# Row statistics move from PSUM to SBUF, the odd heads' attention sums to other PSUM banks, and a quarter of weight granule 47 stays in PSUM

## The chip, the cores and the metric

The kernel runs on one core of one Trainium2 chip. The metric is the device time of one execution in microseconds (us). The kernel before was timed in three runs; their median is 1912.75 us, the lowest 1907.44, the highest 1921.95.

Engines are named as in the profile: PE is TensorE's matmul side and PEld its loading of weights, DVE is VectorE, ACT is ScalarE, POOL is GpSimd and SP is SyncE, which here issues the DMAs of the weights.

## The reference

The result is x + A(xn) + B(xn), where xn is the layer norm of x (2048 rows of 1024 elements, bf16). A is an attention with a recurrent memory: the sequence is cut into 64 segments of 32 rows, and each segment sees 8 memory rows that are the first 8 output rows of the segment before. So the segments can't run side by side.

```python
for s in range(n_seg):                       # 64 segments
    h = concat([mem, xn[:, 32*s:32*(s+1)]])  # 8 memory rows + 32 rows
    q, k, v = (einsum('btd,dhe->bhte', h, W) for W in (Wq, Wk, Wv))   # 32 heads of 128
    scores = einsum('bhqe,bhke->bhqk', q, k) * scale                  # 40 x 40 per head
    p = softmax(where(mask, scores, -1e9))
    o = einsum('bhte,hed->btd', einsum('bhqk,bhke->bhqe', p, v), Wo)
    mem, out_s = o[:, :8], o[:, 8:]
```

B scores each row of xn with a vector w_r, takes the two best rows, sends them through a gated network (weights 1024 x 3584 and 3584 x 1024), scales the result with the sigmoid of the score and adds it to those two rows.

## The kernel before

**Tiling.** The weights of A are cut into 64 granules of 128 x 2048 bf16 (512 KB). Granules 0 to 47 are the projections, in six phases p of eight (kc 0 to 7): q, k of the first 16 heads, q, k of the second 16, v of the first half, v of the second. Granules 48 to 63 are Wo (w = 0 to 15). 44 granules stay in SBUF (tiles wres). Twenty are streamed: read from HBM in every segment, from scratch copies (tiles wsc) that segment 0 makes, into five rotating slots (tile g). The order of the streamed ones is 2, 5, 6, 9, 13, 17, 21, 25, 29, 33, 36, 39, 42, 45, 47, 50, 53, 56, 59, 62. Two of them are partly kept in PSUM: granule 6 whole in two banks, half of 25 in a third (tiles KEPT). After segment 0 granule 6 isn't streamed at all and of 25 only 1024 columns; their kept parts are copied back to SBUF by bring_back (L350) and kept_piece (L354). keep (L333) puts a part into PSUM in segment 0: it turns 128 x 128 blocks on PE, copies them to SBUF, and turns them again.

**Order of the work.** The schedule is manual: every engine executes its instructions in the order in which the code issues them. Within a segment, PE walks through the granules; after each one, after() may issue the next fetch (SP's queue; a fetch waits until the slot's last reader is done), and the hooks stored under (p, kc) are called. A hook at (5,4) thus comes behind the matmuls of granule 44 on every engine's queue. In the hooks stand: transposes of q and k (phase + 1, kc 3), scores(0) at (2,6), exponent and soften(0) at (3,4), scores(1) at (4,6), exponent and soften(1) at (5,0), prep_left at (5,3) in some segments, attend(0,0) at (5,4) and attend(0,1) at (5,6). attend(1,0) and attend(1,1) come at w = 5 and w = 8 of Wo. The 8 last rows of the four segments of a group G (j = s mod 4) are carried on beside as "left" rows: their projections go through PSl (L647), and in segments with j = 3 Wo is also applied to them (WL). prep_left normalises them in segments with j = 3 (sum_left) and j = 0 (norm_left).

**Dependencies.** The code sets no semaphores; the framework derives them from the tiles that each instruction reads and writes.

**PSUM.** There are eight banks of 512 fp32 words per partition. Three hold KEPT. psA has two rotating banks, which phases (PSm) and Wo (WO) take in turn. psL has one for left rows. Two are fixed: BS holds the scores and probabilities (SPS, words 0 to 319), the per-row means and deviations MR (320 to 447) and ML (448 to 479); BT holds the target of transposes (PTB, words 0 to 255) and one set of attention sums (OPB, 256 to 415).

**attend.** attend(half, ph) makes, for four groups of four heads, the sums for two row quarters jl = 0 and 1. The jl = 0 sums go to WO[256:416] in the first half and to BS[0:160] in the second; the jl = 1 sums go to OPB in BT. Then copies (L591, L593) bring each set to OT and to the left rows' tile OTL: all four on ACT in the first half, jl = 0 on ACT and jl = 1 on DVE in the second. After phase 5 the residual (L269) writes WO[0:256] and norm_seg prepares the next segment's rows with MR.

**softmax.** scores (L534, L536 on PE, masks L543, L545, maximum L548, subtraction L549), exponent (L553 on ACT), soften (sum L558, reciprocal L559, products L565, L566, stream transposes L568, L569): all of L543 to L566 read or write BS. two_rows (L239, L240) fetches a mean and a deviation from MR or ML.

Of the kernel before, what the change touches and what calls it, by code (L numbers as in the profile page):

```python
# [8 lines left out]
BF16 = mybir.dt.bfloat16  # L9
F32 = mybir.dt.float32  # L10
# [7 lines left out]
N_RES = 44  # L18
N_SLOT = 5
KEPT_WHOLE = 6  # L20
KEPT_PART = 25
NEG = -30000.0

PHASES = [(0, 0), (1, 0), (0, 1), (1, 1), (2, 0), (2, 1)]
# [3 lines left out]
def kernel(  # L28
# [43 lines left out]

    NG = 64

    streamed = [2, 5, KEPT_WHOLE, 9, 13, 17, 21, KEPT_PART, 29, 33, 36, 39, 42, 45, 47, 50, 53, 56, 59, 62]
    assert len(streamed) == NG - N_RES
    n_str = len(streamed)
    resident = [g for g in range(NG) if g not in streamed]
# [28 lines left out]
    def columns(g, s):  # L107
        if s > 0 and g == KEPT_WHOLE:
            return None
        return slice(0, 1024 if s > 0 and g == KEPT_PART else 2048)  # L110

    wsc = {g: dram.tile([P, columns(g, 1).stop - columns(g, 1).start], BF16, name=f"wsc{g}")
           for g in streamed if g != KEPT_WHOLE}
# [15 lines left out]

    XS = const.tile([P, 256], BF16, name="XS")  # L130
    XN = const.tile([P, 256], BF16, name="XN")
    CT = const.tile([P, 32], F32, name="CT")
    MASK = CT[:, 0:12].bitcast(BF16)
    NEGR = CT[:, 13:14]
    V8 = CT[0:1, 16:24]
    I8 = CT[0:1, 24:32].bitcast(U32)

    BS = psS.tile([P, 512], F32, name="BS")
    BT = psT.tile([P, 512], F32, name="BT")
    SPS = BS[:, 0:8 * NK].rearrange("p (i a k) -> p i a k", i=4, a=2)  # L140
    PTB = BT[:, 0:256].bitcast(BF16)
    OPB = BT[:, 256:256 + 4 * NK]
    MR = BS[:, 320:320 + 2 * NSEG].rearrange("p (s c) -> p s c", c=2)
    ML = BS[:, 448:448 + 2 * NT].rearrange("p (t c) -> p t c", c=2)
    nc.vector.memset(SPS[:, :, :, :], 0.0)
    nc.vector.memset(XN[:, :], 0.0)
    nc.vector.memset(XS[:, :], 0.0)
# [8 lines left out]
    S6 = MISC[:, 704:704 + 24].bitcast(F32).rearrange("p (c s) -> p c s", c=2)  # L156
    RI16 = MISC[:, 728:792].bitcast(F32).rearrange("p (t c) -> p t c", c=2)
    RF = MISC[:, 792:824].bitcast(F32)
    MF = MISC[:, 824:824 + 2 * (XM + 1)].bitcast(F32)
    WRB = MISC[:, 1024:2048]  # L160
    nc.vector.memset(MF, 0.0)
# [35 lines left out]
    def spread(t0, t1):  # L197

        n = t1 - t0
        sd_rows(MV[:, t0:t1, :], VE[:, t0:t1])  # L200
        PD = OPB
        for s in range(5):
            sel = SELM[:, s, :, :].rearrange("p r g -> p (r g)") if s < 4 else SELL.rearrange("p s r g -> p (s r g)")
            nc.tensor.matmul(PD[:, 32 * s:32 * s + 2 * n], lhsT=sel, rhs=MV[:, t0:t1, :].rearrange("p t c -> p (t c)"),
                             start=(s == 0), stop=True, skip_group_check=True)
        for s in range(4):
            mr = MR.rearrange("p (t s) c -> p t s c", s=4)[0:XR4, t0:t1, s, :]
            nc.vector.tensor_copy(out=mr, in_=PD[0:XR4, 32 * s:32 * s + 2 * n].rearrange("p (t c) -> p t c", c=2))
        nc.vector.tensor_copy(out=ML[:, t0:t1, :], in_=PD[:, 128:128 + 2 * n].rearrange("p (t c) -> p t c", c=2))
        nc.vector.tensor_copy(out=RI16[:, t0:t1, 0], in_=MV[:, t0:t1, 0])  # L210
        nc.vector.reciprocal(out=RI16[:, t0:t1, 1], in_=MV[:, t0:t1, 1])

# [16 lines left out]
    def router_top():  # L229
        RROW = home(hx, [1, S], BF16, "RROW")  # L230
        nc.gpsimd.dma_start(out=RROW[:, :], in_=r_d[:, :])
        nc.vector.max(out=V8[:, :], in_=RROW[:, :])
        nc.vector.max_index(out=I8[:, :], in_max=V8[:, :], in_values=RROW[:, :])


    def two_rows(m, tag):
        n = m.shape[0]
        t = one.tile([P, 4], F32, tag=tag, name="RI")[0:n, :]
        nc.vector.tensor_copy(out=t[:, 0:1], in_=m[:, 0:1])  # L239
        nc.vector.reciprocal(out=t[:, 1:2], in_=m[:, 1:2])  # L240
        return t
# [2 lines left out]
        nc.gpsimd.dma_start(out=XN[0:XR4, :], in_=x2[s * SEG:s * SEG + XM, :].rearrange("r (g c) -> (r g) c", g=4))  # L244

    def norm_seg(s):
        mr = two_rows(MR[0:XR4, s, :], "ri")
        ab = mr[:, 2:4]
        xn = XN[0:XR4, :]
        nc.vector.tensor_scalar(out=ab[:, 0:1], in0=mr[:, 1:2], scalar1=1.0, scalar2=None, op0=ALU.add)  # L250
        nc.vector.tensor_scalar(out=ab[:, 1:2], in0=mr[:, 0:1], scalar1=mr[:, 1:2], scalar2=-1.0, op0=ALU.mult, op1=ALU.mult)
        nc.vector.tensor_scalar(out=XS[0:XR4, :], in0=xn, scalar1=ab[:, 0:1], scalar2=ab[:, 1:2],
                                op0=ALU.mult, op1=ALU.add)
        nc.vector.tensor_scalar(out=xn, in0=xn, scalar1=mr[:, 0:1], scalar2=mr[:, 1:2],
                                op0=ALU.subtract, op1=ALU.mult)
# [32 lines left out]
        return t  # L288

    def norm_left(t, G):  # L290
        mr = two_rows(ML[:, G, :], "ri")
        nc.vector.tensor_scalar(out=t[:, :], in0=t[:, :], scalar1=mr[:, 0:1], scalar2=mr[:, 1:2],
                                op0=ALU.subtract, op1=ALU.mult)

    def sum_left(t, G):

        mr = two_rows(ML[:, G, :], "ri")
        nc.vector.tensor_scalar(out=mr[:, 0:1], in0=mr[:, 0:1], scalar1=mr[:, 1:2], scalar2=-1.0,
                                op0=ALU.mult, op1=ALU.mult)
        nc.vector.tensor_scalar(out=mr[:, 1:2], in0=mr[:, 1:2], scalar1=1.0, scalar2=None, op0=ALU.add)  # L300
        nc.vector.tensor_scalar(out=t[:, :], in0=t[:, :], scalar1=mr[:, 1:2], scalar2=mr[:, 0:1],
                                op0=ALU.mult, op1=ALU.add)

    def new_stl(t):
# [7 lines left out]
    queued = []  # L312

    KEPT = [psK.tile([P, 1024], BF16, name=f"KEPT{b}") for b in range(3)]
    KEPT_COLS = {KEPT_WHOLE: {0: KEPT[0][:, 0:512], 1: KEPT[0][:, 512:1024], 2: KEPT[1][:, 0:512], 3: KEPT[1][:, 512:1024]},
                 KEPT_PART: {2: KEPT[2][:, 0:512], 3: KEPT[2][:, 512:1024]}}

    def fetch():
        if not flow:
# [14 lines left out]
    def keep(g, t):  # L334
        for c, K in KEPT_COLS[g].items():
            turned = PTB.rearrange("p (i r) -> p i r", i=4)
            for i in range(4):
                nc.tensor.transpose(out=turned[:, i, :], in_=t[:, 512 * c + P * i:512 * c + P * (i + 1)],
                                    identity=IDENT[:, :])
            XK = one.tile([P, 512], BF16, tag="vl", name="XK")  # L340
            nc.vector.tensor_copy(out=XK[:, :], in_=PTB)
            for i in range(4):
                nc.tensor.transpose(out=K[:, P * i:P * (i + 1)], in_=XK[:, P * i:P * (i + 1)], identity=IDENT[:, :])

# [156 lines left out]
    for s in range(NSEG):  # L501
# [26 lines left out]
        def scores(half):  # L528
            QKL = qkl[0]
            q, k = QT[half], KT[half]  # L530
            for il in range(4):
                for jq in range(4):
                    hh = 4 * il + jq
                    nc.tensor.matmul(SPS[32 * jq:32 * jq + 32, il, 0, :], lhsT=q[:, hh, :], rhs=k[:, hh, :],  # L534
                                     start=(il == 0), stop=True, tile_position=(0, 32 * jq), skip_group_check=True)
                    nc.tensor.matmul(SPS[32 * jq:32 * jq + XL, il, 1, :], lhsT=QKL[:, il, 2 * half, jq, :],  # L536
                                     rhs=k[:, hh, :], start=False, stop=True, tile_position=(0, 32 * jq),
                                     skip_group_check=True)
            for S4, m in ((SPS[:, :, 0, 0:XM], MASK), (SPS[:, :, 0, SEG:NK], None),
                          (SPS[:, :, 1, SEG:NK], MASK[:, 0:XL])):  # L540
                if m is not None:
                    m = m.unsqueeze(1).to_broadcast([P, 4, S4.shape[2]])
                    nc.vector.tensor_tensor(out=S4, in0=S4, in1=m, op=ALU.add)  # L543
                else:
                    nc.vector.tensor_scalar(out=S4, in0=S4, scalar1=NEGR, scalar2=None, op0=ALU.add)  # L545
            S8 = SPS.rearrange("p i a k -> p (i a) k")
            NM = one.tile([P, 8], F32, tag="nm", name="NM")
            nc.vector.tensor_reduce(out=NM[:, :], in_=S8, axis=AX.X, op=ALU.max, negate=True)  # L548
            nc.vector.tensor_tensor(out=S8, in0=S8, in1=NM[:, :].unsqueeze(2).to_broadcast([P, 8, NK]), op=ALU.add)  # L549

# [3 lines left out]

        def soften(half):
            S8 = SPS.rearrange("p i a k -> p (i a) k")
            DN = one.tile([P, 8], F32, tag="nm", name="DN")
            nc.vector.tensor_reduce(out=DN[:, :], in_=S8, axis=AX.X, op=ALU.add)  # L558
            nc.vector.reciprocal(out=DN[:, :], in_=DN[:, :])  # L559
            PT2 = one.tile([P, 2, 4, 64], BF16, tag=("bA", "bE")[half], name="PT2")  # L560
# [11 lines left out]
        def attend(half, ph):  # L572
            if half not in OT:
                OT[half] = one.tile([P, 4, 4, SEG], BF16, tag=("kt", "bC")[half], name="OT")
                if half == 0:
                    nxt["wo"] = psA.tile([P, 512], F32, tag="acc", name="WO")
                sums[half] = [BS[:, 0:4 * NK] if half else nxt["wo"][:, 256:256 + 4 * NK], OPB]
            PTm, PTl = PTs[half]
            for il in range(4):
                for jl in range(2):  # L580
# [43 lines left out]
        if s > 0:  # L624
            hook(0, 0, lambda: bring_back(3, nc.scalar.copy))
            if j in (2, 3):
                hook(0, 1, lambda: bring_back(0, nc.vector.tensor_copy))
            hook(2, 1, lambda: kept_piece(KEPT_PART, 2, nc.vector.tensor_copy))
            hook(2, 2, lambda: kept_piece(KEPT_PART, 3, nc.vector.tensor_copy))
            hook(1, 5, turn_lx)  # L630
        hook(2, 6, lambda: scores(0))
        hook(3, 4, exponent)
# [182 lines left out]
    free_homes += [-1] * N_SLOT  # L815
    fetch_moe()
    assert not moe
    T0 = one.tile([P, 1024], BF16, tag="vl", name="T0")
    XS = T0[0:2, :]
    T1 = one.tile([P, 1024], BF16, tag="otl", name="T1")  # L820
# [107 lines left out]
```

## Time and profile before

| what | value |
|---|---|
| median of 3 runs | 1912.75 us |
| the profiled execution | 1914.95 us |
| its span | 1913.2 us |
| PE busy | 1607.9 us, 84% of the span |
| DVE busy | 906.8 us, 47% |
| ACT busy | 703.0 us, 37% |
| moved by DMA | 712.39 MB, mean 372 GB/s |
| HBM read, written | 694.32 MB, 22.29 MB |
| fetches of whole streamed granules | 1134, each 512 KB |
| fetches of half of granule 25 | 63, each 256 KB |

In the rows that follow, a timeline row gives start, duration, engine, line, operation, tile written <- tiles read, shape, and in brackets the idle time of the engine just before it and what ended it. A group's row gives the count, total busy time and mean duration in ns, and then the idle time before its members. A row of waits gives who waited, for whom, the sum, how often, and the longest. "DMA g<-wsc" is the fetch of a streamed granule. Since matmuls are pipelined, their ends are modelled.

### The profile page before, as it was taken

To read this page: it belongs to the slowest core of one execution; us is meant where nothing else is said; L and a number is where in the kernel's file an instruction comes from. 1 tells how busy PE (TensorE), PEld (TensorE's weight loads), DVE (VectorE), ACT (ScalarE), POOL (GpSimd) and SP (SyncE) were. 2 spreads that over 40 slices of the span, in tenths; PEclk is the share of its full clock that TensorE was granted. 3 is DMA by queue.
4 is the path that set the end of the run, shared out by engine and by line. 5 is a ranking of instruction groups with operands and counts; after the bars stand their busy time and mean duration, and the time that the engine had idled before them with its cause. 6 is when DMAs were issued, how large, how long until landed. Compare 5 with 4: busy or idle time off the path is not lost. (4 is left out here: it accounts for less than half of the span.)

```text
span 1913.2 us, 82718 instructions
## 1 busy us (share of the span) xinstructions
PE 1607.9 (84%) x36320; PEld 891.0 (47%) x36320; DVE 906.8 (47%) x2884; ACT 703.0 (37%) x1886; POOL 294.0 (15%) x590
## 2 busy tenths in 40 slices
PE   3558898888889888989889898989888898889864
PEld 1224545444454445545454554545454544545443
DVE  6824544554455445444554454445444544455430
ACT  1113433443334343434344343334333443343320
POOL 2201111111110211112111111211121111111110
PEclk8669999999999999999999999999999999999995
DMA  9999999999999999999999999999999999999998
GB/s 369 399 363 378 358 381 365 380 379 354 383 352 390 350 382 376 378 381 369 387 353 373 370 372 362 362 387 365 370 363 384 376 366 385 365 386 368 393 390 330
DMA packets 224441, 712.39 MB, mean 372 GB/s; under 512 B 33664, under 2 KB 44464, under 8 KB 224080
## 3 DMA queue, kind: packets, MB, share of 16 engines
q1 hardware_dynamic: 194384, 671.18, 92.9%
q0 software_dynamic: 21056, 28.07, 4.4%
q10 hardware_dynamic: 8640, 7.87, 1.2%
q8 instruction: 283, 4.64, 0.9%
q14 instruction: 78, 0.64, 0.1%
HBM read 694.32 MB, written 22.29 MB: 375 GB/s over the span
## 5 line engine op out<-in xcount | busy, mean ns | idle before, releaser
L669 PE MATMUL PSm<-wres,ST 128*32 128x512 bf16 x8448 | 720.2, 385 | 21.2 <-DVE ST L283 6.7
L669 PEld LDWEIGHTS <-ST 128*32 128x32 bf16 x12288 | 325.8, 96 | 396.4 <-issue 166.9
L669 PE MATMUL PSm<-g,ST 128*32 128x512 bf16 x3588 | 362.4, 387 | 88.5 <-DMA g<-wsc 60.3
L685 ACT CAST XB<-PSm 128x512 bf16<-128x512 f32 x256 | 150.0, 586 | 306.9 <-PE PSm L669 305.3
L730 PEld LDWEIGHTS <-OT 128*32 128x32 bf16 x8192 | 214.1, 97 | 104.1 <-issue 80.8
L730 PE MATMUL WO<-wres,OT 128*32 128x256 bf16 x5632 | 237.2, 275 | 14.0 <-issue 8.9
L647 PE MATMUL PSl<-wres,STL 128*32 128x512 bf16 x2112 | 200.3, 390 | 1.5 <-issue 1.4
L526 DVE COPY KT<-BT 128x512 bf16<-128x512 bf16 x128 | 52.5, 410 | 307.7 <-ACT XB L685 148.9
L458 POOL DMA_DIRECT2D LX<-ql_d x63 | 33.8, 537 | 937.6 <-ACT OTL L593 525.0
L730 PE MATMUL WO<-g,OT 128*32 128x256 bf16 x2560 | 131.2, 279 | 54.4 <-DMA g<-wsc 42.0
L793 POOL DMA_DIRECT2D out_dram<-XN x256 | 129.6, 514 | 228.0 <-DVE XN L791 219.1
L707 ACT CAST VM<-PSm 128x512 bf16<-128x512 f32 x128 | 77.0, 602 | 153.5 <-PE PSm L669 121.5
L350 ACT COPY BK<-KEPT 128x512 bf16<-128x512 bf16 x126 | 78.3, 621 | 96.9 <-PE WO L730 96.9
L521 ACT COPY QT<-BT 128x512 bf16<-128x512 bf16 x128 | 75.0, 586 | 105.3 <-PE BT L516 99.7
L647 PEld LDWEIGHTS <-STL 128*32 128x32 bf16 x3072 | 85.1, 98 | 57.7 <-issue 8.0
L584 PEld LDWEIGHTS <-VM 32*128 32x128 bf16 x2048 | 67.6, 91 | 93.0 <-issue 71.3
L516 PEld LDWEIGHTS <-XB 128*128 128x128 bf16 x1024 | 58.5, 98 | 106.1 <-ACT XB L685 76.7
L543 DVE TENSOR_TENSOR BS<-BS,CT 128x96 f32<-128x96 f32 (+1 forms) x256 | 59.7, 233 | 100.8 <-PE BS L536 96.3
L354 DVE COPY g<-KEPT 128x512 bf16<-128x512 bf16 x126 | 47.6, 420 | 122.5 <-PE PSm L669 70.2
L791 DVE CAST XN<-WO 128x256 bf16<-128x256 f32 x64 | 27.2, 425 | 160.7 <-PE WO L730 160.7
L516 PE MATMUL BT<-IDENT,XB 128*128 128x128 bf16 x1024 | 102.0, 222 | 1.4 <-ACT QKL L476 1.4
L558 DVE TENSOR_REDUCE DN<-BS 128x8 f32<-128x320 f32 x128 | 63.0, 492 | 67.2 <-ACT BS L553 67.2
(168 smaller groups left out, 2382.2 us busy)
## 6 DMA issues: line engine op xcount, KB each, us to landing
g<-wsc SPq DMA_DIRECT2D x1134, 512.0 KB, 6.1
g<-wsc SPq DMA_DIRECT2D x63, 256.0 KB, 5.5
LX<-ql_d POOLq DMA_DIRECT2D x63, 128.0 KB, 6.0
ql_d<-XBl ACTq DMA_DIRECT2D x60, 128.0 KB, 5.6
MW<-in_B_w_gate_dram SPq DMA_DIRECT2D x16, 448.0 KB, 9.2
MW<-in_B_w_up_dram SPq DMA_DIRECT2D x16, 448.0 KB, 9.1
wres<-in_A_Wk_dram SPq DMA_DIRECT2D x12, 512.0 KB, 14.3
MW<-in_B_w_down_dram SPq DMA_DIRECT2D x12, 512.0 KB, 10.2
```

What stands on the lines that cost most here:

```text
L350: copy(out=back[c][:, :], in_=KEPT_COLS[KEPT_WHOLE][c])
L516: nc.tensor.transpose(out=PTq[:, il, :, :].rearrange("p j r -> p (j r)"), in_=XB[:, il * P:(il + 1) * P], identity=IDENT[:, :])
L521: nc.scalar.copy(out=QT[half][:, :, :], in_=pv)
L543: nc.vector.tensor_tensor(out=S4, in0=S4, in1=m, op=ALU.add)
L558: nc.vector.tensor_reduce(out=DN[:, :], in_=S8, axis=AX.X, op=ALU.add)
L584: nc.tensor.matmul(o, lhsT=VM[half][q0:q0 + 32, il * P:(il + 1) * P], rhs=PTm[q0:q0 + 32, il, 0:NK], start=True, stop=False, tile_position ...
L647: nc.tensor.matmul(PSl[32 * jq:32 * jq + 32, :], lhsT=STL[:, g % KC, :], rhs=part(Gv, jq), start=first_, stop=last_, tile_position=(0, 32 ...
L669: nc.tensor.matmul(PSm[32 * jq:32 * jq + 32, :], lhsT=ST[:, kc, :], rhs=part(Gv, jq), start=(kc == 0), stop=(kc == KC - 1), tile_position= ...
L685: nc.scalar.copy(out=XB[:, :], in_=PSm[:, :])
L707: nc.scalar.copy(out=VM[half][:, :], in_=PSm[:, :])
L730: nc.tensor.matmul(PS[32 * g:32 * g + 32, 0:256], lhsT=lhs(h), rhs=Gv[:, D * hs + 256 * g:D * hs + 256 * (g + 1)], start=False, stop=(last ...
L793: nc.gpsimd.dma_start(out=out2[s * SEG:s * SEG + XM, 256 * g:256 * (g + 1)], in_=OB[32 * g:32 * g + XM, :])
```

## The change

Four things change together.

- MR leaves BS. The statistics of segments 1 to 63 lie in SBUF as bf16 (MRS, in the tile CT), those of segment 0 in MR0; ML stays in BS, but as bf16 in 16 words (480 to 495). The small tiles of two_rows and of the softmax (RI, NM, DN) become fixed places in CT. The two best scores and their places wait in BS (TOP, words 496 to 511) until the end.
- OPB moves from BT to BS[320:480].
- attend's sums: jl = 0 go to OPB in both halves; jl = 1 go to WO[256:416] in the first half and to a bank of their own from psA (SUM) in the second. Which engine copies which jl stays.
- The freed 256 words of BT keep the last quarter of granule 47 as bf16. In segment 0 keep puts it there; from segment 1 on the fetch of 47 brings 1536 of its 2048 columns, and a DVE copy at (4,5) brings the rest.

```diff
-KEPT_PART = 25
+KEPT_PARTS = {25: (2, 3), 47: (3,)}
...
-        return slice(0, 1024 if s > 0 and g == KEPT_PART else 2048)
+        return slice(0, 2048 - 512 * len(KEPT_PARTS.get(g, ())) if s > 0 else 2048)
...
-    CT = const.tile([P, 32], F32, name="CT")
+    CT = const.tile([P, 25 + NSEG - 1], F32, name="CT")
...
+    MRS = CT[:, 13:13 + NSEG - 1].bitcast(BF16).rearrange("p (s c) -> p s c", c=2)
+    RI = CT[:, 12 + NSEG:16 + NSEG]
+    NM = CT[:, 16 + NSEG:24 + NSEG]
...
-    OPB = BT[:, 256:256 + 4 * NK]
-    MR = BS[:, 320:320 + 2 * NSEG].rearrange("p (s c) -> p s c", c=2)
-    ML = BS[:, 448:448 + 2 * NT].rearrange("p (t c) -> p t c", c=2)
+    OPB = BS[:, 320:320 + 4 * NK]
+    ML = BS[:, 480:480 + NT].bitcast(BF16).rearrange("p (t c) -> p t c", c=2)
+    TOP = BS[0:1, 496:512]
...
-    def two_rows(m, tag):
-        n = m.shape[0]
-        t = one.tile([P, 4], F32, tag=tag, name="RI")[0:n, :]
+    def two_rows(m):
+        t = RI[0:m.shape[0], :]
...
-        mr = two_rows(MR[0:XR4, s, :], "ri")
+        mr = two_rows(MRS[0:XR4, s - 1, :] if s else MR0[0:XR4, :])
...
+    KEPT_COLS = {47: {3: BT[:, 256:512].bitcast(BF16)}, KEPT_WHOLE: {0: KEPT[0][:, 0:512], 1: KEPT[0][:, 512:1024], 2: KEPT[1][:, 0:512], 3: KEPT[1][:, 512:1024]},
...
-            NM = one.tile([P, 8], F32, tag="nm", name="NM")
...
-            DN = one.tile([P, 8], F32, tag="nm", name="DN")
+            DN = NM
...
-                sums[half] = [BS[:, 0:4 * NK] if half else nxt["wo"][:, 256:256 + 4 * NK], OPB]
+                beside = psA.tile([P, 512], F32, tag="acc", name="SUM")[:, 0:4 * NK] if half else nxt["wo"][:, 256:256 + 4 * NK]
+                sums[half] = [OPB, beside]
...
+            hook(4, 5, lambda: kept_piece(47, 3, nc.vector.tensor_copy))
...
+    T3 = one.tile([P, 16], F32, tag="bA", name="T3")
+    V8 = T3[0:1, 0:8]
+    I8 = T3[0:1, 8:16].bitcast(U32)
+    nc.vector.tensor_copy(out=V8, in_=TOP[:, 0:8])
+    nc.vector.tensor_copy(out=I8, in_=TOP[:, 8:16])
```

More of the change, by code (lines that the diff above doesn't have):

```diff
@@ L73 @@
     NG = 64
-    streamed = [2, 5, KEPT_WHOLE, 9, 13, 17, 21, KEPT_PART, 29, 33, 36, 39, 42, 45, 47, 50, 53, 56, 59, 62]
+    streamed = [2, 5, KEPT_WHOLE, 9, 13, 17, 21, 25, 29, 33, 36, 39, 42, 45, 47, 50, 53, 56, 59, 62]
     assert len(streamed) == NG - N_RES
@@ L131 @@
     XN = const.tile([P, 256], BF16, name="XN")
-    CT = const.tile([P, 32], F32, name="CT")
+    CT = const.tile([P, 25 + NSEG - 1], F32, name="CT")
     MASK = CT[:, 0:12].bitcast(BF16)
-    NEGR = CT[:, 13:14]
-    V8 = CT[0:1, 16:24]
-    I8 = CT[0:1, 24:32].bitcast(U32)
+    NEGR = CT[:, 12:13]
+    MRS = CT[:, 13:13 + NSEG - 1].bitcast(BF16).rearrange("p (s c) -> p s c", c=2)
+    RI = CT[:, 12 + NSEG:16 + NSEG]
+    NM = CT[:, 16 + NSEG:24 + NSEG]
     BS = psS.tile([P, 512], F32, name="BS")
@@ L158 @@
     RF = MISC[:, 792:824].bitcast(F32)
+    MR0 = MISC[:, 880:882]
+    MLT = MISC[:, 884:884 + 2 * NT]
     MF = MISC[:, 824:824 + 2 * (XM + 1)].bitcast(F32)
@@ L206, in spread @@
         for s in range(4):
-            mr = MR.rearrange("p (t s) c -> p t s c", s=4)[0:XR4, t0:t1, s, :]
-            nc.vector.tensor_copy(out=mr, in_=PD[0:XR4, 32 * s:32 * s + 2 * n].rearrange("p (t c) -> p t c", c=2))
-        nc.vector.tensor_copy(out=ML[:, t0:t1, :], in_=PD[:, 128:128 + 2 * n].rearrange("p (t c) -> p t c", c=2))
+            pd = PD[0:XR4, 32 * s:32 * s + 2 * n].rearrange("p (t c) -> p t c", c=2)
+            if t0 == 0 and s == 0:
+                nc.vector.tensor_copy(out=MR0[0:XR4, :], in_=pd[:, 0, :])
+                pd = pd[:, 1:, :]
+            if pd.shape[1]:
+                a = 4 * (t0 + (t0 == 0 and s == 0)) + s - 1
+                nc.vector.tensor_copy(out=MRS[0:XR4, a:a + 4 * (pd.shape[1] - 1) + 1:4, :], in_=pd)
+        nc.vector.tensor_copy(out=MLT[:, 2 * t0:2 * t1], in_=PD[:, 128:128 + 2 * n])
+        nc.vector.tensor_copy(out=BS[:, 480 + t0:480 + t1], in_=MLT[:, 2 * t0:2 * t1].bitcast(F32))
         nc.vector.tensor_copy(out=RI16[:, t0:t1, 0], in_=MV[:, t0:t1, 0])
@@ L231, in router_top @@
         nc.gpsimd.dma_start(out=RROW[:, :], in_=r_d[:, :])
+        V8 = home(hm, [1, 8], F32, "V8")
+        I8 = home(resident[-3], [1, 8], U32, "I8")
         nc.vector.max(out=V8[:, :], in_=RROW[:, :])
         nc.vector.max_index(out=I8[:, :], in_max=V8[:, :], in_values=RROW[:, :])
-    def two_rows(m, tag):
-        n = m.shape[0]
-        t = one.tile([P, 4], F32, tag=tag, name="RI")[0:n, :]
+        nc.vector.tensor_copy(out=TOP[:, 0:8], in_=V8[:, :])
+        nc.vector.tensor_copy(out=TOP[:, 8:16], in_=I8[:, :])
+    def two_rows(m):
+        t = RI[0:m.shape[0], :]
         nc.vector.tensor_copy(out=t[:, 0:1], in_=m[:, 0:1])
@@ L290, in norm_left @@
     def norm_left(t, G):
-        mr = two_rows(ML[:, G, :], "ri")
+        mr = two_rows(ML[:, G, :])
         nc.vector.tensor_scalar(out=t[:, :], in0=t[:, :], scalar1=mr[:, 0:1], scalar2=mr[:, 1:2],
@@ L295, in sum_left @@
     def sum_left(t, G):
-        mr = two_rows(ML[:, G, :], "ri")
+        mr = two_rows(ML[:, G, :])
         nc.vector.tensor_scalar(out=mr[:, 0:1], in0=mr[:, 0:1], scalar1=mr[:, 1:2], scalar2=-1.0,
@@ L314 @@
     KEPT = [psK.tile([P, 1024], BF16, name=f"KEPT{b}") for b in range(3)]
-    KEPT_COLS = {KEPT_WHOLE: {0: KEPT[0][:, 0:512], 1: KEPT[0][:, 512:1024], 2: KEPT[1][:, 0:512], 3: KEPT[1][:, 512:1024]},
-                 KEPT_PART: {2: KEPT[2][:, 0:512], 3: KEPT[2][:, 512:1024]}}
+    KEPT_COLS = {47: {3: BT[:, 256:512].bitcast(BF16)}, KEPT_WHOLE: {0: KEPT[0][:, 0:512], 1: KEPT[0][:, 512:1024], 2: KEPT[1][:, 0:512], 3: KEPT[1][:, 512:1024]},
+                 25: {2: KEPT[2][:, 0:512], 3: KEPT[2][:, 512:1024]}}
     def fetch():
@@ L339, in keep @@
                                     identity=IDENT[:, :])
-            XK = one.tile([P, 512], BF16, tag="vl", name="XK")
+            XK = one.tile([P, 512], BF16, tag="bx" if "vl" in group else "vl", name="XK")
             nc.vector.tensor_copy(out=XK[:, :], in_=PTB)
@@ L627 @@
                 hook(0, 1, lambda: bring_back(0, nc.vector.tensor_copy))
-            hook(2, 1, lambda: kept_piece(KEPT_PART, 2, nc.vector.tensor_copy))
-            hook(2, 2, lambda: kept_piece(KEPT_PART, 3, nc.vector.tensor_copy))
+            hook(2, 1, lambda: kept_piece(25, 2, nc.vector.tensor_copy))
+            hook(2, 2, lambda: kept_piece(25, 3, nc.vector.tensor_copy))
+            hook(4, 5, lambda: kept_piece(47, 3, nc.vector.tensor_copy))
             hook(1, 5, turn_lx)
```

## The prediction

> **What bounds the kernel now.** First the page, to see which resource is full:
>
> ```profile
> span 1913.2 us, 82718 instructions
> PE 1607.9 (84%) x36320; PEld 891.0 (47%) x36320; DVE 906.8 (47%) x2884; ACT 703.0 (37%) x1886; POOL 294.0 (15%) x590
> ...
> DMA  9999999999999999999999999999999999999998
> ...
> q1 hardware_dynamic: 194384, 671.18, 92.9%
> ...
> L669 PE MATMUL PSm<-g,ST 128*32 128x512 bf16 x3588 | 362.4, 387 | 88.5 <-DMA g<-wsc 60.3
> ...
> L730 PE MATMUL WO<-g,OT 128*32 128x256 bf16 x2560 | 131.2, 279 | 54.4 <-DMA g<-wsc 42.0
> ...
> g<-wsc SPq DMA_DIRECT2D x1134, 512.0 KB, 6.1
> ```
>
> The DMA engines are busy in every slice, and a granule lands 6.1 us after its issue; yet PE shows only 60.3 + 42.0 = 102.3 us of waiting for streamed granules, 1.62 us in each of 63 segments. So DMA and PE run close to each other, and a saving on one side counts only up to where the other takes over. Next the windows, cut near the middle of segment 25 and where segment 26 begins (columns: stretch, length, busy time of PE, PEld, DVE, ACT, POOL, clock, DMA share, GB/s):
>
> ```profile
> 799.00:816.00 17.00, 15.39 (x410) 8.87 (x402) 10.76 (x35) 7.20 (x22) 0.54 (x1) 1.00 1.01 386
> 816.00:826.00 10.00, 8.64 (x138) 3.59 (x130) 1.84 (x6) 3.54 (x7) 2.71 (x6) 1.00 0.98 363
> ```
>
> The second part of a segment moves 386 GB/s and the first part of the next 363: the transfers set the pace late in a segment, where streamed granules stand closer together, and have some slack early.
>
> Then the order of work around attend(0,0), segment 25 (timelines of DVE, PE and ACT):
>
> ```profile
> 804.29 0.39 DVE L526 COPY KT<-BT 128x512 bf16<-128x512 bf16 x1
> 805.23 0.27 DVE L543 TENSOR_TENSOR BS<-BS,CT 128x96 f32<-128x96 f32 x1 [0.56 <-PE BS L536]
> 807.58 0.49 DVE L558 TENSOR_REDUCE DN<-BS 128x8 f32<-128x320 f32 x1 [0.49 <-ACT BS L553]
> 808.68 0.21 DVE L566 TENSOR_TENSOR OTL<-BS,DN 128x64 bf16<-128x64 f32 x1
> ...
> 807.20 0.19 PE L584 MATMUL BT<-PT,VM 32*128 32x40 bf16 x1
> 809.29 0.31 PE L269 MATMUL WO<-XS,IDENT 128*32 128x256 bf16 x4 [0.20 <-ACT OTL L593]
> ...
> 807.12 0.42 ACT L553 ACTIVATE BS<-BS 128x320 f32<-128x320 f32 x1 [1.03 <-DVE BS L549]
> 808.93 0.30 ACT L593 CAST OTL<-WO 128x32 bf16<-128x32 f32 x1
> 809.23 0.31 ACT L593 CAST OTL<-BT 128x32 bf16<-128x32 f32 x1
> ```
>
> Two things are to be seen. PE starts the first half's attention sums at 807.20, into BT, while ACT (from 807.12) and DVE (until 808.68 + 0.21 = 808.89) still work on the second half's scores in BS. And PE's residual, which writes words 0 to 255 of WO, starts at 809.29, 0.06 us after ACT has read words 256 to 415 of the same WO (808.93 + 0.30 = 809.23): a write waits for a read of **other words of the same PSUM tile**.
>
> **The change part by part.**
>
> *The lighter transfer.* Granule 47 is read in 1536 of 2048 columns in 63 segments: 128 KB less each. At the 386 GB/s of the late part, where it lands, that is 131072 / 386e3 = 0.34 us, 21 us in all. It is worth this only where PE waits for DMA afterwards.
>
> *Its copy from PSUM.* The trace has the same copy for granule 25, and the pieces of keep for the once-only turning in segment 0:
>
> ```profile
> L354 DVE COPY g<-KEPT 128x512 bf16<-128x512 bf16 x126 | 47.6, 420 | 122.5 <-PE PSm L669 70.2 <-DMA g<-wsc 31.1 <-PE PSl L647 21.2
> L343 PE MATMUL KEPT<-IDENT,XK 128*128 128x128 bf16 x24 | 3.0, 264 | 5.7 <-DVE XK L341 5.7
> L338 PE MATMUL BT<-IDENT,g 128*128 128x128 bf16 x24 | 2.9, 258 | 0.0
> ```
>
> One copy is 0.42 us. It stands on DVE's queue between the copy to KT, which ends at 804.29 + 0.39 = 804.68, and the first mask at 805.23, which waits for PE's scores: a gap of 0.55 us hides it. Its slot was granule 33's, which PE has passed before the transposes that KT waits for; so it finds nothing to wait for. Without that cover, masks, softmax and what follows come 0.1 to 0.4 us later per segment, 6 to 25 us; I take 0 and keep 10 for the range. Turning the piece in segment 0 costs (3.0 + 5.7 + 2.9) / 6 pieces = 1.9 us of PE, under the loads of the weights, and that segment also copies 128 KB less to the scratch; together I take 0, with 2 us either way.
>
> *Odd heads' sums.* attend(0,0) writes jl = 0 into BS instead of WO, and jl = 1 into WO instead of BT. OPB and SPS are views of the one tile BS. If the wait seen in WO holds here, PE can't start before the last read of BS that stands earlier in the program: ACT's exponential and all of DVE's softmax up to L566; in the segments with j = 3 and j = 0 also the two reads of ML in BS (L239, L240) that prep_left puts at (5,3), behind two stream transposes. Segment 25 above, and the next three (for each the DVE read that ends last and PE's start):
>
> ```profile
> 835.97 0.21 DVE L566 TENSOR_TENSOR OTL<-BS,DN 128x64 bf16<-128x64 f32 x1
> 834.34 0.19 PE L584 MATMUL BT<-PT,VM 32*128 32x40 bf16 x1
> ...
> 863.45 0.15 DVE L240 RECIPROCAL RI<-BS 128x1 f32<-128x1 f32 x1
> 860.86 0.19 PE L584 MATMUL BT<-PT,VM 32*128 32x40 bf16 x1
> ...
> 890.73 0.15 DVE L240 RECIPROCAL RI<-BS 128x1 f32<-128x1 f32 x1
> 889.36 0.19 PE L584 MATMUL BT<-PT,VM 32*128 32x40 bf16 x1
> ```
>
> With 0.06 us from a read's end to PE's start, the new stall is 808.89 + 0.06 - 807.20 = **1.75** us in segment 25 (j = 1), 1.90 in 26 (j = 2), 2.80 in 27 (j = 3) and 1.58 in 28 (j = 0): 2.01 on the mean. The row of L269 shows ACT as the reader. If only ACT held PE up, the stall would end with the exponential, 807.12 + 0.42 + 0.06 - 807.20 = 0.40 us. The code names no engine in this, so I take the long value and keep 0.40 for the range. [...]
>
> Behind the waiting matmul on PE's queue are granules 45 and 47, the rest of attend(0), the residual and all of Wo. ACT's copies of the sums and of VM wait for PE, and so does SP, whose next fetches need the slots that PE frees.
>
> *The order in WO.* ACT now copies the sums in BS first and those in WO second, so the residual waits for the last of its four copies: 809.23 + 0.31 = 809.54 instead of 809.23, another **0.31** us. Where PE comes later anyway it costs less, at the least nothing.
>
> *What covers it.* A late PE doesn't wait where it waited before. PE's waits from attend(0,0) to about 6 us into the next segment, from the waits in these four stretches (us in total, times, longest):
>
> ```profile
> PE PSm L669 <- DMA g<-wsc: 1.3, 3, 0.7
> PE WO L730 <- DMA g<-wsc: 0.8, 2, 0.7
> PE BS L584 <- ACT VM L707: 0.4, 1, 0.4
> ...
> PE WO L730 <- DMA g<-wsc: 1.8, 3, 0.8
> PE PSm L669 <- DMA g<-wsc: 0.4, 1, 0.4
> ...
> PE WL L269 <- DVE VL L712: 0.7, 1, 0.7
> ...
> PE WO L730 <- DMA g<-wsc: 1.0, 2, 0.8
> ...
> 805.00 0.40 PE L669 MATMUL PSm<-g,ST 128*32 128x512 bf16 x4
> 805.21 0.40 PE L669 MATMUL PSm<-wres,ST 128*32 128x512 bf16 x4
> ```
>
> The last two rows show what a wait hides: a set of four matmuls counts as busy for 0.40 us, but the next starts after 0.21, so each listed wait is about 0.19 us longer than its idle time. Stall (with the 0.31) against cover: segment 25: 2.06 against 1.3 + 0.8 + 0.4 + 5 x 0.19 = 3.45, nothing left; 26: 2.21 against 2.2 + 4 x 0.19 = 2.96, nothing left; 27: 3.11 against 0.7, 2.4 left; 28: 1.89 against 1.0 + 2 x 0.19 = 1.38, 0.5 left. Where cover is left over (25 and 26), DMA still sets the end and the 0.34 counts. The four together: 2.4 + 0.5 - 2 x 0.34 = 2.2 us, or 0.56 per segment, **35 us** in 63.
>
> Against that stands the mean of the run, from its list of waits:
>
> ```profile
> PE PSm L669 <- DMA g<-wsc: 60.3, 125, 1.3
> ...
> PE WO L730 <- DMA g<-wsc: 42.0, 104, 1.2
> ```
>
> 1.62 us of waits, plus 0.19 x (125 + 104) / 63 = 0.69, is 2.31 per segment against a stall of 2.01 + 0.31 = 2.32. Were all of it usable, nothing would remain of the stall and nothing of the gain: 0, and with the extra 0.31 gone as well -20. It isn't all usable: a part lies ahead of the attention, and segment 27, with the longest stall and WL's second set of projections, has hardly any. I take +23, two thirds of the way from 0 to 35.
>
> *The rest.* two_rows reads SBUF instead of PSUM, NM and DN share one place: small DVE operations of 0.1 to 0.2 us each, with norm_seg off PE's path; 0. The top-two copies through PSUM are a few such operations once, in segment 0 and beside the last weights' loads; 0, at most 1 us.
>
> **The sum.** 1914.95 (the profiled execution, 1.75 above its span) + 23 = 1938; the median of the three runs is 2.2 lower, so against it **1936**. One per cent, 19 us, is about what a measurement tells from no change, as the three runs themselves spread over 14.5 us.
>
> **The rivals.**
>
> 1. *DMA swallows the stall* (other side: not slower). If DMA is the bound over the whole cycle, the 2.3 us only take the place of PE's waits, and each segment ends 0.34 us earlier: 1912.75 - 21 = 1892. For it: the full DMA row, and 2.31 against 2.32. Against it: PE waits for no granule in segment 27's list. It decides where cover exceeds 2.32 + 0.34 us in nearly every segment. 0.12; with cover just meeting the stall, 1903 to 1922, another 0.15.
> 2. *No wait arises* (disjoint words of BS aren't ordered, or DVE doesn't count and the stall is 0.40, wholly covered): also 1892. The L269 row speaks against the first. 0.05.
> 3. *The stall is hardly covered.* A late PE frees slots late, SP issues late, and DMA idles in turn, so that waits come back further on: from half of 2.32 x 63 = 146 us less the relief, 1912.75 + 73 - 21 = 1965, towards 1990. For it: the first part of a segment, at 363 GB/s, already isn't full. Against it: 6.1 us to landing, at 512 KB / 386e3 = 1.36 us for one granule, means about four in flight, far more than 2.8 us of stall. 0.15.
> 4. *The change doesn't do what it says:* the copy into granule 47's slot waits for that granule's own transfer and blocks DVE's queue. Landing after 6.1 instead of 0.55 us would delay the masks by 5.5 us per segment, 346 us: 2260. Some of L354's idle time ends with a DMA (31.1 us), but the copies for granule 25 don't take that long. 0.03.
>
> The forecast itself has 0.50, with 1922 to 1955 as its own range.
>
> **How the numbers follow.** Below 1894 lie most of rivals 1 (its first half) and 2: faster 0.10. Above 1932 lie three quarters of the forecast and rivals 3 and 4: slower 0.55. The rest, 0.35, is within 1%. The range from 1897 to 1970 leaves out about 0.1 on each side.
>
> **What would show it.** Right: the first L584 of attend(0,0) writes BS 0.06 us behind L566 (j = 1, 2) or L240 (j = 3, 0), with PE idle some 1.5 to 3 us before it; L269 follows ACT's last copy; the waits for g<-wsc in L730 fall well below 42 us; q1 moves 8 MB less, and DMA's share drops under that of before. Wrong: L584 starts while DVE still reads BS; the waits of L730 stay; the L354 copy at (4,5) ends after the first mask could start; or the segments with j = 3 are not the ones that grow.

## The result and the profile after

The changed kernel takes 2048.7 us (median of 4 runs, 2045.6 to 2050.7) against 1913.9 us: a ratio of **1.070, 95% interval 1.066 to 1.075**, 135 us slower. The profiled execution has a span of 2044.0 us. The forecast had the sign, but not the size; the measured time lies far above its range of 1897 to 1970, and above the 1990 up to which its third rival reached.

The lines of the page of the changed kernel that answer to those shown of before:

```profile
span 2044.0 us, 82818 instructions
PE 1649.5 (81%) x36328; PEld 919.5 (45%) x36328; DVE 928.0 (45%) x2954; ACT 698.3 (34%) x1886; POOL 292.8 (14%) x590
...
DMA  9999999999999999999999999999999999999998
...
q1 hardware_dynamic: 194384, 662.92, 89.6%
...
L682 PE MATMUL PSm<-g,ST 128*32 128x512 bf16 x3588 | 369.5, 396 | 105.5 <-DMA g<-wsc 88.5
...
L596 PE MATMUL BS<-PT,VM 32*128 32x40 bf16 x1024 | 94.2, 181 | 131.6 <-DVE CT L252 80.8
```

q1 moves 8.3 MB less, as it should, but the span is 131 us longer. The last row is the new stall: PE sits idle for 131.6 us ahead of attend's sums in BS, 10.0 us of them once, in segment 0. Note the DMA row: nines in all slices but the last, as before, although the mean rate has fallen from 372 to 344 GB/s. A slice is 51 us long, almost two segments, and a 9 stands for 90% or more, so the row hides stretches as slack as those shown below, at 68 to 82%; it doesn't say that the transfers are what the others wait for.

The list of waits of the changed kernel (us in total, times, longest), who held PE:

```profile
PE PSm L682 <- DMA g<-wsc: 88.5, 125, 2.8
PE BS L596 <- DVE CT L252: 80.8, 31, 10.0
...
PE BS L596 <- DVE OTL L577: 50.8, 33, 2.1
PE WO L281 <- ACT OTL L605: 22.9, 59, 0.5
...
PE WO L743 <- DMA g<-wsc: 4.5, 12, 0.7
```

Before, the residual's row was this:

```profile
PE WO L269 <- ACT OTL L593: 4.6, 23, 0.2
```

In 33 segments the stall ends with DVE's L577, the last product of the softmax (L566 before), in 31 with L252, the read of ML (L240 before). The waits for granules in Wo have nearly vanished (42.0 before, 4.5 now). But those in the projections have grown from 60.3 to 88.5. The new copy of granule 47's last quarter never waits, neither for PE nor for its own transfer:

```profile
L366 DVE COPY g<-BT 128x512 bf16<-128x512 bf16 x63 | 25.8, 409 | 0.0
```

Segment 27 (j = 3) in both timelines and in five stretches. First the end of the stall, DVE's row and PE's:

```profile
916.31 0.15 DVE L252 RECIPROCAL CT<-BS 128x1 f32<-128x1 bf16 x1
...
916.51 0.17 PE L596 MATMUL BS<-PT,VM 32*128 32x40 bf16 x1 [3.22 <-DVE CT L252]
```

PE starts 0.05 us behind DVE's last read of BS. Now the windows up to the middle of the stall, in the rest of it, to the point where the clock changes, while it is changed, and to the segment's end (length, busy PE, PEld, DVE, ACT, POOL, clock, DMA share, GB/s):

```profile
896.30:914.60 18.30, 16.41 (x298) 7.77 (x299) 8.30 (x25) 6.16 (x13) 3.56 (x7) 0.91 1.01 371
914.60:916.50 1.90, 0.00 (x0) 0.00 (x0) 1.76 (x9) 0.00 (x0) 0.00 (x0) 1.00 1.01 386
916.50:917.80 1.30, 1.19 (x32) 0.62 (x32) 0.71 (x3) 0.77 (x4) 0.00 (x0) 0.99 0.68 274
917.80:921.20 3.40, 3.13 (x62) 2.32 (x65) 1.78 (x7) 1.19 (x5) 0.00 (x0) 0.50 0.74 196
921.20:926.60 5.40, 5.40 (x190) 4.33 (x182) 2.06 (x7) 2.03 (x7) 0.52 (x1) 1.00 0.82 269
```

Here two things are to be seen that the prediction hadn't. While PE stands still, DMA goes on at 386 GB/s for a while, but then falls to 274, 196 and 269: the transfers that were already issued run out, and new ones are issued only as PE frees slots: in this segment's trace SP issues no fetch between 913.22 and 917.26 us. SP's queue bears this out over the whole run; before, and then with the change, it waited for PE's projections and for PE's Wo:

```profile
SPq L327 <- PE PSm L669: 446.9, 593, 2.7
...
SPq L327 <- PE WO L730: 136.8, 249, 1.8
```

```profile
SPq L339 <- PE PSm L682: 552.5, 612, 4.0
...
SPq L339 <- PE WO L743: 200.4, 249, 1.8
```

And 1.3 us after the stall **PE's clock falls to 0.50 for 3.4 us**. A set of eight matmuls of Wo then takes about twice as long: the next set starts 0.43 us later in the slow stretch and 0.23 us later after it.

```profile
919.97 0.67 PE L743 MATMUL WO<-g,OT 128*32 128x256 bf16 x8
920.40 0.67 PE L743 MATMUL WO<-wres,OT 128*32 128x256 bf16 x8
...
921.97 0.40 PE L743 MATMUL WO<-g,OT 128*32 128x256 bf16 x8
922.20 0.39 PE L743 MATMUL WL<-g,OTL 128*32 128x256 bf16 x8
```

In the trace of the changed kernel the clock stands at 0.5 in 45 stretches, 181 us together, leaving out the first 150 us and one long stretch behind the last segment; before it was 4 stretches and 17 us. 39 of the 45 begin between 0.9 us before and 2.8 us after the start of attend(0,0). The mean granted clock:

```profile
core 0: 2044.0 us, clock 0.924
```

It was 0.961 before. After segment 0, all 15 segments in which PE was idle for 2.39 us or more ahead of attend(0,0) saw such a stretch, and 22 of the 38 with 1.3 to 2.4 us. What decides between these can be read from the same trace: in it every change of the clock lies on a grid of 3.41 us, and each of the 45 stretches is one or two steps of it long. Of the steps at full clock between 160 and 1700 us, all 20 in which PE was busy for less than 47% of the time were followed by a slow one, 16 of 52 with 47 to 65%, and none of 336 with more (busy time by the modelled ends of the matmuls). So in this trace it counts how much of an idle time falls into one step.

### The profile page after: what moved, and what is told of

It reads as the page before. It is cut to its first block, busy times and chain, and to the rows that moved or that the text cites. A ratio compares the mean times of both kernels' runs of the same rounds, so it can differ in the third digit from the quotient of the medians.

```text
span 2044.0 us, 82818 instructions
## 1 busy us (share of the span) xinstructions
PE 1649.5 (81%) x36328; PEld 919.5 (45%) x36328; DVE 928.0 (45%) x2954; ACT 698.3 (34%) x1886; POOL 292.8 (14%) x590
## 3 DMA queue, kind: packets, MB, share of 16 engines
q1 hardware_dynamic: 194384, 662.92, 89.6%
## 5 line engine op out<-in xcount | busy, mean ns | idle before, releaser
L682 PE MATMUL PSm<-g,ST 128*32 128x512 bf16 x3588 | 369.5, 396 | 105.5 <-DMA g<-wsc 88.5
L743 PE MATMUL WO<-wres,OT 128*32 128x256 bf16 x5632 | 265.1, 305 | 5.0 <-DMA wres<-in_A_Wo_dram 3.2
L743 PEld LDWEIGHTS <-OT 128*32 128x32 bf16 x8192 | 231.1, 106 | 45.9 <-issue 21.0
L596 PE MATMUL BS<-PT,VM 32*128 32x40 bf16 x1024 | 94.2, 181 | 131.6 <-DVE CT L252 80.8
L603 ACT CAST OT<-BS 128x128 bf16<-128x128 f32 x256 | 67.9, 265 | 368.9 <-PE WO L598 187.9
L743 PE MATMUL WO<-g,OT 128*32 128x256 bf16 x2560 | 142.2, 299 | 11.8 <-DMA g<-in_A_Wo_dram 6.8
L598 PEld LDWEIGHTS <-VL 32*128 32x128 bf16 x2048 | 71.6, 94 | 138.8 <-issue 138.7
L596 PEld LDWEIGHTS <-VM 32*128 32x128 bf16 x2048 | 75.1, 93 | 92.5 <-issue 88.2
L603 DVE CAST OT<-SUM 128x128 bf16<-128x128 f32 x128 | 37.3, 291 | 145.2 <-PE SUM L598 145.2
```

Of the source, the lines that this page charges most:

```text
L596: nc.tensor.matmul(o, lhsT=VM[half][q0:q0 + 32, il * P:(il + 1) * P], rhs=PTm[q0:q0 + 32, il, 0:NK], start=True, stop=False, tile_position ...
L598: nc.tensor.matmul(o, lhsT=group["vl"][q0:q0 + 32, c0:c0 + P], rhs=PTl[q0:q0 + 32, il, 0:NK], start=False, stop=True, tile_position=(q0, 0 ...
L603: copy(out=OT[half][:, 2 * ph + jl, :, :], in_=ov[:, :, 0:SEG])
L682: nc.tensor.matmul(PSm[32 * jq:32 * jq + 32, :], lhsT=ST[:, kc, :], rhs=part(Gv, jq), start=(kc == 0), stop=(kc == KC - 1), tile_position= ...
L743: nc.tensor.matmul(PS[32 * g:32 * g + 32, 0:256], lhsT=lhs(h), rhs=Gv[:, D * hs + 256 * g:D * hs + 256 * (g + 1)], start=False, stop=(last ...
```

## The experiments

After the result three causes were open for 135 us: the stall with the slow clock (A), the stall with DMA running dry (B), and something else in the change. A ratio is always to the kernel before, on the same chip.

**The stall taken away (e1), and the lighter transfer with it (e2).** BT's words 0 to 159 are free in phase 5, so the first half's jl = 0 sums can go there:

```diff
-                sums[half] = [OPB, beside]
+                sums[half] = [OPB if half else BT[:, 0:4 * NK], beside]
```

> The changed kernel, but the first half's jl = 0 sums go to BT, words 0 to 159 (free at that time), instead of BS; nothing else differs. All theories in which the wait for BS is the cause (the stall with the clock, or the stall with starved DMA): PE starts attend(0,0) without the wait of about 2 us, PE's clock falls to half no more often than before (4 stretches after the first 150 us, against 45 in the changed kernel), and the time is 1892 if the lighter transfer counts whole (-21 us), up to 1914 if it counts for nothing. If something else in the change is the cause (SUM in the rotating banks, the DVE copy at (4,5)), it stays above 1990.

> The same as e1_sums_in_bt, but granule 47 is streamed whole as before. This leaves the moved statistics, SUM, and BT for the first half: 1908 to 1920, the time before. The difference to e1_sums_in_bt is what the lighter transfer is worth without a stall: 21 us if DMA sets the pace in every segment, 10 to 15 if in half of them, under 5 if PE does.

e1: 1926.0 us, ratio 1.0066 (1.0035 to 1.0097). e2: 1934.4 us, 1.0094 (1.0065 to 1.0124). In e1's list of waits no L596 waits for DVE's softmax any more, and the clock is 0.952; it is at half in 11 stretches, 41 us together, not in 4 as was expected. So the wait for BS is the cause of about 122 of the 135 us. But 12 us remain in a kernel that has no stall and moves less, 20 us in the one that moves as much as before. Both lie outside what was expected: a third cause is left. The lighter transfer is worth 8 us here by the medians, 5 by the ratios, not 21, and the intervals overlap.

**PE kept busy during the stall (e3).** The work fills the gap, and its result is overwritten by the residual and the sums:

```diff
             PTm, PTl = PTs[half]
+            if half == 0 and ph == 0:
+                for n in range((7, 6, 6, 12)[j]):
+                    for jq in range(4):
+                        nc.tensor.matmul(nxt["wo"][32 * jq:32 * jq + 32, :], lhsT=ST[:, n % KC, :],
+                                         rhs=res_tiles[44][:, 512 * jq:512 * (jq + 1)], start=True, stop=True,
+                                         tile_position=(0, 32 * jq), skip_group_check=True)
```

> The changed kernel, with 6 or 7 sets (12 where j = 3) of four matmuls on PE ahead of attend(0,0), 1.3 to 2.6 us of work whose result isn't used, just long enough to fill most of the stall. Theory A (the idle PE is put to half clock for 3.4 us, 181 us in all against 17 before, and that costs up to half of the 164 us and eats the cover): half clock falls below 60 us and the time falls by 50 to 82 us, to 1965 to 2000. Theory B (a PE that frees its slots late starves DMA, the clock is a side effect): the time stays within 10 us of 2049, whatever the clock does.

2022.5 us, ratio 1.057 (1.054 to 1.060). The clock's mean is 0.954, 51 us in slow stretches, counted as above. PE is as late as in the changed kernel, but awake:

```profile
PE PSm L688 <- DMA g<-wsc: 80.9, 126, 2.4
...
PE BS L602 <- DVE CT L252: 17.5, 15, 10.7
...
PE BS L602 <- DVE OTL L577: 11.4, 25, 0.8
```

Of the 17.5 us in the second row 10.7 are segment 0. Both theories miss: the clock costs about 1.31% or **25 us**, by the intervals 15 to 35, neither 50 to 82 nor nothing. The larger part, 5.0% between e1 and e3 or 96 us, is the late PE itself. The wait in segment 0 has little part in this: attend(0,0) of segment 1 starts at 151.3 us in e1's trace and at 151.8 in e3's.

**The changed kernel without the lighter transfer (e4).** Granule 47 is streamed whole:

```diff
-KEPT_PARTS = {25: (2, 3), 47: (3,)}
+KEPT_PARTS = {25: (2, 3)}
...
-            hook(4, 5, lambda: kept_piece(47, 3, nc.vector.tensor_copy))
```

> The changed kernel with granule 47 streamed whole, so with the stall but without the lighter transfer and the DVE copy. If the stall has made PE the bound: 2045 to 2057, the lighter transfer worth under 8 us. If DMA still sets the pace (theory B): 2065 to 2072, 21 us more.

2049.5 us, ratio 1.072 (1.068 to 1.076) against 1.070 (1.066 to 1.075): with the stall in place, 8.3 MB less and the DVE copy together make no difference that can be measured. This is the first branch: under the stall it isn't the amount of the transfers that sets the pace.

**The order of the sums (e5, e6).** e1 still has the jl = 0 sums outside WO, so that the residual waits for ACT's last copy. e5 turns them round:

```diff
-                sums[half] = [OPB if half else BT[:, 0:4 * NK], beside]
+                sums[half] = [OPB, beside] if half else [beside, BT[:, 0:4 * NK]]
```

> As e1_sums_in_bt, but in the first half jl = 0 goes to WO and jl = 1 to BT, the order of before; so ACT frees WO two copies earlier and the residual needn't wait for the last of them. Theory order (the residual's wait is what e1_sums_in_bt still loses): the stretch from attend(0,0) to the residual falls by 0.2 to 0.3 us, the time by 13 to 20 us, to 1906 to 1913. Theory other (moved statistics, SUM, or DVE's extra copy cost it): within 5 us of e1_sums_in_bt's 1926.

> As e5_wo_first, with granule 47 streamed whole: what is left of the change are the moved statistics and SUM. Theory order: 1912 to 1918, the time before. Theory other: 1925 to 1935. The difference to e5_wo_first is again the lighter transfer alone: 8 us by the first pair, 21 if DMA set the pace everywhere.

e5: 1932.7 us, 1.0062 (1.0037 to 1.0087); e6: 1930.1 us, 1.0064 (1.0039 to 1.0088), where the kernel before took 1919.5 on that chip. The theory of the order falls. Nor does this pair show a gain from the lighter transfer: 0.0002 between the ratios. The residual's wait did shrink, from e1's row to e5's:

```profile
PE WO L281 <- ACT OTL L605: 26.2, 60, 0.5
```

```profile
PE WO L281 <- ACT OTL L605: 7.7, 39, 0.2
```

But 18.5 us of PE's waiting went and the time stayed: these 0.3 us are covered. And e6, which has nothing of the change left but the moved statistics with the longer CT and the other places of the sums, SUM among them, still loses 0.64%.

**PE made late (e7).** e5 with three sets of the extra matmuls, range(3), ahead of each attend(0,0).

> As e5_wo_first, with 3 sets of four matmuls (0.65 us of PE, result not used) ahead of each attend(0,0): PE comes 0.65 us later in 64 segments, 41 us, but is never idle, so the clock stays. Theory cover (a late PE only loses waits it had anyway, 1.6 us and more per segment): 0 to 8 us above e5_wo_first. Theory starved DMA (slots come free later, so the transfers come later by as much): 30 to 41 us above.

1957.6 us, ratio 1.0198 (1.0167 to 1.0229), 24.9 us above e5, of 41 us inserted: 60% comes through. Between the two theories, nearer to starved DMA.

**prep_left behind the attention (e8).**

```diff
-            hook(5, 3, prep_left)
+            hook(5, 7, prep_left)
```

> The changed kernel with prep_left at (5,7) instead of (5,3), behind attend(0,0) and attend(0,1) on all queues. If the reads of ML in BS (behind two stream transposes) are what makes the stall longer where j = 3 and j = 0: the stall there falls by 0.9 us where j = 3 (3.26 to about 2.3) and by 0.3 to 0.9 where j = 0, about 20 to 35 us in all with what the clock adds: 2014 to 2030. If not, 2045 to 2052.

2013.1 us, ratio 1.050 (1.047 to 1.053), 2.0% or 38 us less than the changed kernel. The stall no longer ends with a read of ML:

```profile
PE BS L596 <- DVE OTL L577: 58.4, 45, 2.2
PE BS L596 <- DVE BX L577: 30.4, 16, 2.3
...
PE BS L596 <- DVE BS L246: 11.9, 1, 11.9
```

The last row is segment 0. Without that segment it is 88.8 us of idle PE instead of 121.6, and the mean distance from the matmul before to attend(0,0) falls from 3.26 to 2.25 us where j = 3 and from 2.15 to 1.22 where j = 0. With the clock (0.930 against 0.924) the gain is slightly more than was expected.

**The third cause: where the slots lie (e9, e10, e11).** A 4096-byte packet of a granule took 160 ns or less in 88% of all cases before, but in 56 to 63% in every one of these kernels with the change (counted from the trace's packets of q1 between 160 and 1700 us). What all of these share is the longer table CT, 88 words instead of 32, which stands ahead of the streamed slots in SBUF: they begin 224 bytes further on in each partition, at byte 198880 instead of 198656. The shift follows from the sizes of CT; the addresses themselves stand in no trace. e11 is the kernel before with nothing but a longer CT; e9 is e5, and e10 the changed kernel, with the slots back in their place (CT keeps 32 words, the other statistics go behind all tiles):

```diff
-    CT = const.tile([P, 32], F32, name="CT")
+    CT = const.tile([P, 72], F32, name="CT")
```

```diff
-    CT = const.tile([P, 25 + NSEG - 1], F32, name="CT")
+    CT = const.tile([P, 32], F32, name="CT")
+    CU = rest.tile([P, NSEG - 8], F32, name="CU")
```

> The kernel before with one edit: CT has 72 words instead of 32, of which 40 are unused, so that every slot g starts 160 bytes further on. Nothing else of the change is in it. Theory address: the share of quick packets falls from 88% to about 56 to 63% and the time rises by 8 to 15 us, ratio 1.004 to 1.008. Theory statistics: ratio 1.000, within 0.2%.

> As e5_wo_first (no stall, the order of before, the lighter transfer), but the larger table of statistics no longer stands ahead of the streamed slots in SBUF: CT keeps its 32 words, 56 words of statistics go behind all other tiles, so every slot g starts again at byte 198656, as before, and not 224 bytes further. Theory address (in before 88% of the 4096-byte packets took 160 ns or less, in every kernel with the longer CT 56 to 63%): the share returns to about 88%, the 12 us that e5_wo_first and e6_wo_first_no47 lose vanish and the lighter transfer shows: ratio to before 0.987 to 1.000. Theory statistics (the moved statistics or SUM cost it): ratio 1.004 to 1.009 as in e5_wo_first.

> The changed kernel with its slots back at byte 198656, by the same edit: the stall stays. Theory address: 8 to 15 us faster than the changed kernel, ratio to before 1.062 to 1.066. Theory statistics: ratio 1.068 to 1.073 as measured.

e11: 1930.0 us, ratio **1.0058** (1.0031 to 1.0086): an unused 160 bytes per partition cost 11 us. Its share of quick packets is 71%, higher than was expected, and its page shows the same packets and bytes as before:

```profile
span 1934.3 us, 82718 instructions
...
q1 hardware_dynamic: 194384, 671.18, 92.8%
```

92.8% of 16 x 1934.3 us over 194384 packets is 147.8 ns for one, counting all sizes; before it was 92.9% of 16 x 1913.2, 146.3 ns.

e9: 1910.3 us, ratio **0.9958** (0.9933 to 0.9983), 88% quick packets: without the stall and with its slots in place the rest of the change is 8 us faster than before, and 1.04% faster than e5. e10: 2038.9 us, 1.0618 (1.0570 to 1.0665), 0.8% below the changed kernel, about as expected, though the two intervals touch; its share is 86%. So the theory of the statistics falls: it is the place of what lies behind CT. CT moves everything behind it; that the streamed slots are what counts is argued from the packets alone. Only shifts of 160 and 224 bytes were run, and why the place matters isn't shown.

**As late as the stall, but awake and in place (e12).** e9 with nine sets, range(9), ahead of each attend(0,0).

> As e9_aligned, with 9 sets of four matmuls (1.94 us of PE, result not used) ahead of each attend(0,0): PE is late by about what the stall made it, 124 us in 64 segments, but never idle, so the clock stays. Theory cover (only what exceeds the waits for DMA costs): 20 to 45 us above e9_aligned. Theory starved DMA (in e7_plus3 25 of 41 us came through, 60%): 75 to 110 us above.

1998.7 us, 88.5 us above e9, of 124 us inserted: 71%. What PE waits for granules in e9, and then in e12:

```profile
PE PSm L687 <- DMA g<-wsc: 61.5, 118, 1.9
...
PE WO L748 <- DMA g<-wsc: 33.0, 73, 2.2
```

```profile
PE PSm L693 <- DMA g<-wsc: 61.5, 94, 2.1
...
PE WO L754 <- DMA g<-wsc: 27.1, 41, 2.0
```

94.5 us against 88.6: a PE that comes 1.94 us later in every segment still waits nearly as long for its granules. SP's queue tells why, first in e9, then in e12:

```profile
SPq L344 <- PE PSm L687: 460.2, 608, 2.8
SPq L344 <- DMA g<-wsc: 320.7, 578, 2.7
```

```profile
SPq L344 <- PE PSm L693: 574.1, 612, 6.2
SPq L344 <- DMA g<-wsc: 258.8, 425, 2.6
```

The fetches wait 114 us longer for the matmuls of the projections to free their slots, so they are issued later.

## Why the prediction was right or wrong

The 135 us come apart by differences of ratios, times 1914 us: 96 the late PE (e3 against e1), 25 the clock (the changed kernel against e3), 20 the place of the slots (e5 against e9; e10 gives 16, and e11 gives 11 for 160 bytes), less 8 for what the rest gains (e9). By the intervals each of these has an error of some 5 to 10 us, so that they add up to 133 is partly luck. The order of the sums is within the error (e1 against e5).

- **The new stall: right.** The prediction had 1.75, 1.90, 2.80 and 1.58 us, 2.01 on the mean. In the traces the mean distance between the matmul before and attend(0,0)'s first (segments 4 to 59) grows from 0.31 us to 1.93, 1.96, 3.26 and 2.15, that is by 2.01. The single stalls were off by up to 0.26 us both ways (1.62, 1.65, 2.95 and 1.84), so that the mean agrees so closely is partly luck. DVE's reads of BS held PE up (it starts 0.05 us behind the last of them in segment 27) as ACT's read of WO did before (0.06 us in segment 25), so 1.75 and not 0.40 was the value; the rows are L596 waiting for L252 (80.8 us) and for L577 (50.8 us). The share of ML was right too (e8).
- **What covers it: wrong, and this is the main failure.** The prediction set the stall against PE's waits for DMA as though the transfers kept coming while PE stood still. They do for a while (386 GB/s in the last 1.9 us of segment 27's stall), then the rate falls to 274 and 196, and SP's queue shows fetches waiting longer for PE to free a slot (552.5 us against 446.9 before, and 574.1 in e12 against 460.2 in e9). The waits vanish in Wo (42.0 to 4.5 us) and come back in the next segment (60.3 to 88.5). Where it was measured with PE awake, 60 to 76% of the delay came through (25 of 41 us in e7, 88 of 124 in e12, and 96 in e3 of about 127, its delay over e1 being 2.01 us in 63 segments); the prediction let 0.37 of 2.32 us through, 16%, two thirds of the way between two sums that both took the waits as free. This is rival 3, which had a chance of 0.15 and a price that began at half of the stall. Where the rest of the delay is won back isn't shown.
- **A term was missing: the clock.** PE's idle time brought the granted clock down to 0.50 for 3.4 or 6.8 us, in 39 segments: 25 us. The trace of before has 4 such stretches too, but nothing that the prediction showed of it said that a stall of 2 us at this place would bring them on. In the changed kernel's trace steps of 3.41 us in which PE was busy for up to 65% were followed by it, and idle times from 1.46 to 3.22 us (twice 0.6 to 0.7) were enough.
- **A second missing term: the table ahead of the slots.** The longer CT was counted as nothing. It moved every slot by 224 bytes, which costs 16 to 20 us (e10, e9).
- **The lighter transfer: too dear.** 21 us were forecast for full effect; 5 to 8 us was measured at best (e2 to e1), nothing in the other pair (e6 to e5) and nothing under the stall (e4). That it is so little without a stall isn't explained by these runs; with the slots in place it wasn't tried alone.
- **The copy at (4,5): right.** Its row shows 0.0 us of idle time before it, so it waited for nothing, and the first masks behind it still wait for PE's scores.
- **The order in WO: right as a wait, wrong as a price.** The residual's wait grew from 4.6 to 22.9 us in the list, as the step had it, but 0.31 us per segment was added to the stall; without the stall it costs nothing (e5).
- **Rivals 1, 2 and 4** didn't come: the stall was there, it wasn't swallowed, and DVE's queue wasn't blocked.

## What to carry to other kernels

A wait for DMA on an engine's list is not free room for a stall of that engine: where the same engine frees the buffers, a stall moves the transfers too; here only 24 to 40% of it was covered. Ask of every new bank or tile for a result who else still reads it at this point of the program; here the same sums in a free part of another bank, with the table out of the slots' way, made the difference between 7% slower and 0.4% faster. And ask of every table that grows what lies behind it in SBUF.

## What the runs showed of the hardware that was not expected

- PE's granted clock fell to 0.50 for stretches of 3.4 or 6.8 us after idle times of PE well below that: 15 of 15 segments with at least 2.39 us of idle, 22 of 38 with 1.3 to 2.4 us. In the changed kernel's trace it changes on a grid of 3.41 us, and a slow step followed all 20 steps with PE busy below 47%, 16 of 52 with 47 to 65%, none of 336 above. Filling the idle time with useless matmuls gave 25 us back (e3).
- 160 unused bytes per partition ahead of the streamed slots cost 0.58% (0.31 to 0.86%) of the time, and the share of 4096-byte packets of 160 ns or less fell from 88 to 71% (e11).
- The DMA row of the page reads 9 in all slices but the last at 372 and at 344 GB/s alike.
